# Moving loads to ScalarE's queue and stores to SyncE's in a planned attention-and-mixer kernel, with later assumed transposes, a third output buffer and no TensorE turning

## The chip, the cores and the metric

One core of one Trainium2 chip runs the whole program. The metric is device time in microseconds of one execution, inputs and outputs in HBM. The medians are of several executions. All executions here carry the state "fast" (one core, no other core to disturb it); the kernel before nevertheless spreads over 17 us, and that spread turns out to be part of the story.

Names used: PE is TensorE (PEld its weight loads), DVE is VectorE, ACT is ScalarE, POOL is GpSimd, SP is SyncE.

## The reference

Eight batches of a gated attention without softmax, followed by a mixer:

```python
# batch 8, S = 3136, D = 256, d_qk = 64, rank 32, hidden 1024
scores = z @ z.T / S                       # symmetric, per batch
x      = u * (maximum(scores, 0)**2 @ v)
h      = (x.T @ U @ V).T                   # low-rank mixing over the sequence
uu     = x + h
out    = uu + maximum(uu @ w_ch1, 0) @ w_ch2
```

The scores are symmetric, so a 128x128 block computed for (row, column) serves (column, row) once it is transposed. Most blocks are transposed by DMA, on SP.

## The kernel before

The program is planned in Python before it is built. Every piece of work is a task with engines, an assumed duration and an assumed latency. A small simulation of the engines picks at each moment which task each engine takes, and the resulting order is emitted. The engines run it in order and wait on semaphores. So a changed assumption costs nothing by itself: it changes the order of the same work.

```python
LQ = "SP"; SQ = "POOL"            # queues of loads and stores
TURNED = tuple(range(8,16))       # batch 0: block rows that TensorE transposes
Z_AT1 = 2; V_AT1 = 5              # column of batch 0 after which z, v of batch 1 are fetched
AT24_0 = 6                        # place of the tail column in batch 0
L_PE, L_EW, L_TR, L_DMA = 0.36, 0.08, 1.3, 2.2   # assumed latencies; L_TR: DMA transpose
LTR0 = 1.0                        # more of it in batch 0
...
x = add(f"tr{b}.{c}.{t0}", {"SP": t_tr(nt)}, ..., pipe=TB * nt,
        lat=L_TR + (LTR0 if b == 0 and c >= 8 else 0.0))     # transpose by DMA
...
add(f"st{b}.{k}.{h}", {SQ: 0.6 if SQ == "POOL" else 0.45} if b < NB - 1 else {"SP": 0.5}, ...)
...
def gate_v(self, t, v):           # POOL: one element, holds back the three cast loads of v (batch 0)
    i = self.nc.gpsimd.tensor_copy(out=w[:1, NT // 2, :1], in_=w[:1, 2 * GATE_V, :1])
```

Half of batch 0's v is loaded by three POOL DMAs that cast to bf16 on the way; both kernels do so. `gate_v` waits until the first v piece is cast, so that these loads don't compete with the first z and v.

## Time and profile before

| | before |
|---|---|
| median of the first three runs | 1040.89 us (1038.57 to 1045.36) |
| profiled execution | 1035.29 us, span 1033.5 us |
| TensorE busy, idle | 1011.2 us, 22.3 us |
| idle TensorE in the first 75 us | 8.8 us |
| DVE, ACT, POOL busy | 590.8, 498.9, 73.0 us |

The busy share of TensorE counts a matmul from its start to its modelled end, so it includes filling and draining. "Granted clock" is the share of TensorE's full clock that the chip let it run at. The page says where TensorE is idle, and the table of stretches says when. Those lines are in the prediction below.

### The profile page before, as it was taken

Reading aid. Unit: us, or ns where it says so; the run is one execution under the profiler, and the core shown is the slowest. Engines: PE = TensorE matmul, PEld = TensorE weight load, DVE = VectorE, ACT = ScalarE, POOL = GpSimd, SP = SyncE. Lnnn points to the kernel's source line nnn. Section 1 sums busy time; section 2 is a strip of 40 time slices with the busy share of each in tenths; the row PEclk is TensorE's granted clock in tenths of the full one; section 3 lists DMA queues with packets and bytes.
Section 4 is the critical chain, followed back from the end, with each engine's and each line's share of the span. In section 5 each row is a group of like instructions: output and inputs, shape, how many; then the busy total and the mean of one; then the engine's idle time right before and its main releaser. Section 6 shows DMA issues by size and latency. Waiting matters only on the chain.

```text
span 1033.5 us, 22358 instructions
## 1 busy us (share of the span) xinstructions
PE 1011.2 (98%) x9164; PEld 749.7 (73%) x9243; DVE 590.8 (57%) x1054; ACT 498.9 (48%) x614; POOL 73.0 (7%) x137
## 2 busy tenths in 40 slices
PE   8899999999999999999999999999999999999998
PEld 5578777777777777777677777677767777678765
DVE  8796754457645646465564656565654565443352
ACT  7664554544454445453463445544454453552343
POOL 1060000000000000001000000000000000000000
PEclk9899999999999999999999999999999999999999
DMA  9989998889888888897897979889898789663152
GB/s 214 182 218 212 153 197 199 188 176 171 178 202 177 181 152 188 189 202 153 158 194 179 199 170 179 165 206 199 145 181 200 185 167 180 130 129 89 39 123 83
DMA packets 408103, 176.41 MB, mean 171 GB/s; under 512 B 369824, under 2 KB 373216, under 8 KB 408000
## 3 DMA queue, kind: packets, MB, share of 16 engines
q1 hardware_dynamic: 400112, 151.32, 73.3%
q0 software_dynamic: 7600, 23.27, 6.9%
q8 instruction: 72, 1.18, 0.5%
q10 hardware_dynamic: 288, 0.39, 0.1%
q14 instruction: 31, 0.25, 0.1%
HBM read 60.70 MB, written 25.69 MB: 84 GB/s over the span
## 4 chain that ended last, share of the span: by engine, by line
PE 92%; DMA 4%; DVE 2%; issue 1%; ACT 1%; SPq 0%; POOL 0%; DVEq 0%; POOLq 0%; ACTq 0%
PE acc L1124 47%; PE acc L1268 16%; PE pair L1242 15%; PE pair L1087 7%; PE acc L1134 2%; DMA uT<-ubf 1%; DMA q<-q 1%; PE acc L1139 1%; PE pair L1204 1%; DVE q L1108 1%; PE acc L1166 1%; PE acc L1261 1%; DMA us<-in_u_dram 0%; DVE q L1215 0%; DMA stg<-in_moe_U_dram 0%
## 5 line engine op out<-in xcount | busy, mean ns | idle before, releaser
L1124 PE MATMUL acc<-v,q 128*128 128x256 bf16 x4632 | 569.2, 273 | 5.0 <-DMA q<-TJ 1.8
L1124 PEld LDWEIGHTS <-q 128*128 128x128 bf16 x4632 | 441.8, 98 | 121.2 <-issue 41.7
L1102 ACT ACTIVATE q<-pair 128x1024 bf16<-128x1024 f32 (+7 forms) x268 | 217.8, 863 | 183.4 <-PE pair L1087 180.4
L1253 ACT ACTIVATE r<-pair 128x1024 bf16<-128x1024 f32 (+1 forms) x191 | 187.4, 1009 | 193.1 <-PE pair L1242 184.4
L1108 DVE TENSOR_TENSOR q<-q 128x1024 bf16<-128x1024 bf16 (+7 forms) x392 | 211.6, 579 | 10.1 <-ACT q L1102 8.3
L1268 PE MATMUL acc<-w2b,r 128*128 128x256 bf16 x1536 | 181.6, 273 | 0.6 <-DVE xc L1157 0.6
L1157 DVE TENSOR_TENSOR xc<-acc,us 128x256 bf16<-128x256 f32 x192 | 80.9, 422 | 171.3 <-PE acc L1134 83.9
L1242 PE MATMUL pair<-uT,w1b 128*128 128x512 bf16 (+1 forms) x711 | 165.8, 350 | 5.9 <-DMA uT<-ubf 2.1
L1268 PEld LDWEIGHTS <-r 128*128 128x128 bf16 x1536 | 148.7, 98 | 26.9 <-issue 6.9
L1104 DVE TENSOR_SCALAR q<-pair 128x768 bf16<-128x768 f32 (+6 forms) x124 | 119.4, 968 | 79.5 <-PE pair L1087 72.6
L1242 PEld LDWEIGHTS <-w1b 128*128 128x128 bf16 x896 | 78.9, 98 | 70.2 <-issue 6.8
L917 POOL DMA_DIRECT2D out_dram<-ob x98 | 53.4, 545 | 860.1 <-DVE ob L1280 776.8
L1087 PE MATMUL pair<-zT 64*128 64x384 bf16 (+4 forms) x952 | 99.7, 313 | 0.9 <-DVE q L1104 0.4
L1280 DVE TENSOR_TENSOR ob<-acc,u 128x512 f32<-128x512 f32 (+1 forms) x91 | 60.0, 659 | 62.2 <-PE acc L1268 61.9
L1215 DVE TENSOR_TENSOR u<-pair,xc 128x1024 f32<-128x1024 f32 x42 | 50.8, 1219 | 11.9 <-PE pair L1204 11.9
L1087 PEld LDWEIGHTS <-zT 64*128 64x128 bf16 x952 | 35.3, 95 | 30.5 <-issue 20.8
L943 ACT CAST ubf<-u 128x1024 bf16<-128x1024 f32 x25 | 26.2, 1046 | 49.6 <-DVE u L1215 38.1
L947 DVE CAST v<-stg 128x512 bf16<-128x512 f32 (+1 forms) x58 | 24.2, 418 | 41.5 <-DMA stg<-in_v_dram 41.5
L943 ACT CAST v<-stg 128x512 bf16<-128x512 f32 (+1 forms) x40 | 24.2, 605 | 33.5 <-DMA stg<-in_v_dram 33.0
L1134 PE MATMUL acc<-v,q 64*128 64x256 bf16 (+1 forms) x168 | 26.9, 277 | 0.0
L1242 PE MATMUL pair<-q,w1b 128*128 128x512 bf16 (+1 forms) x106 | 22.0, 351 | 1.6 <-DVE q L1215 1.0
L973 ACT ACTIVATE zbf<-stg 128x512 bf16<-128x512 f32 (+1 forms) x26 | 15.3, 613 | 11.6 <-DMA stg<-in_z_dram 11.6
(78 smaller groups left out, 242.8 us busy)
## 6 DMA issues: line engine op xcount, KB each, us to landing
us<-in_u_dram SPq DMA_DIRECT2D x96, 256.0 KB, 3.4
stg<-in_v_dram SPq DMA_DIRECT2D x90, 256.0 KB, 3.6
out_dram<-ob POOLq DMA_DIRECT2D x84, 256.0 KB, 3.4
q<-q SPq DMA_TRANSPOSE x356, 3.3
stg<-in_z_dram SPq DMA_DIRECT2D x22, 256.0 KB, 3.3
out_dram<-ob SPq DMA_DIRECT2D x12, 256.0 KB, 2.0
stg<-in_moe_w_ch_dram SPq DMA_DIRECT2D x8, 256.0 KB, 4.1
v<-in_v_dram POOLq DMA_DIRECT2D x3, 256.0 KB, 8.6
```

Source lines behind the costliest of these rows:

```text
L917: i = self.q_of(t).dma_start(out=out, in_=in_)
L1087: self.nc.tensor.matmul(out=ps[:, h, pc : pc + w], lhsT=z[a, r * P : (r + 1) * P], rhs=z[a, c0 : c0 + w], start=True, stop=True,)
L1102: self.nc.scalar.activation(out=o, in_=i, func=AF.Relu)
L1104: self.nc.vector.tensor_single_scalar(out=o, in_=i, scalar=0.0, op=ALU.max)
L1108: self.nc.vector.tensor_tensor(out=o, in0=o, in1=o, op=ALU.mult)
L1124: self.nc.tensor.matmul(out=self.acc[acc.i][:, d0 : d0 + D], lhsT=self.q[:, ref.i, :], rhs=self.v[v.i][:, j, :], start=first and n == 0, s ...
L1157: self.nc.vector.tensor_tensor(out=o, in0=i0, in1=i1, op=ALU.mult)
L1215: self.nc.vector.tensor_tensor(out=o, in0=i, in1=x, op=ALU.add)
L1242: self.nc.tensor.matmul(out=o, lhsT=self.w1b[:, e, ht * P : (ht + 1) * P], rhs=r, start=e == 0, stop=e == ND - 1)
L1253: self.nc.scalar.activation(out=o, in_=i, func=AF.Relu)
L1268: self.nc.tensor.matmul(out=self.acc[acc.i][:, w * D : (w + 1) * D], lhsT=self.r1[r1s[ht // 2].i][:, ht % 2, (2 * h + w) * P : (2 * h + w ...
L1280: self.nc.vector.tensor_tensor(out=o, in0=i, in1=x, op=ALU.add)
```

## The change

The intent: take load issues off SP, where transposes are issued, put stores there instead of on POOL, and let the plan expect transposes later. Several settings were retuned with it.

```diff
-LQ = "SP"
-SQ = "POOL"
-DIRECT = (0, 20, 16, 20)
+LQ = "ACT"
+SQ = "SP"
+DIRECT = (0,20,16,20,22)
-TURNED = tuple(range(8,16))
-W_AT = 6
+W_AT = 5
-Z_AT1 = 2
-V_AT1 = 5
+Z_AT1 = 7
+V_AT1 = 7
-AT24_0 = 6
+AT24_0 = 4
-LTR0 = 1.0
-LOOK = 8
+LTR0 = 2.0
+L_TR = 2.5
+LOOK = 10
-NEAR = 1
+NEAR = 3
-HOLD = 0.06
+HOLD = 0.03
 ... (Z_AT 5 to 4, TOKS 5 to 6; buffers: "ob" 2 to 3, score blocks 296 to 288; one small memset doubled)
-                    f"zt{b}.{p}", {"PE": 0.06 * nb}, ...
+                    f"zt{b}.{p}", {"PE": (0.056 if b else 0.107) * nb}, ...
 ... (the branch for TURNED, turn_quad and copy_quad are removed)
```

More of the change, by code (lines that the diff above doesn't have):

```diff
@@ L21 @@
 ZSCALE = 1.0 / math.sqrt(float(S))
-NBLK = 296
 NXC = 7
+NUS = 3
+NSTG = 6
+NUT = 2
+NR1 = 7
+NOB = 3
+NBLK = 296 - 8 * (NXC + NUS + NSTG + NUT + NR1 + NOB - 27)
 NPAIR, NACC = 3, 2
-LQ = "SP"
-SQ = "POOL"
-DIRECT = (0, 20, 16, 20)
+LQ = "ACT"
+SQ = "SP"
+DIRECT = (0,20,16,20,22)
 FLIP = 16
+ZB = 1
 WARM = 22
-TURNED = tuple(range(8,16))
-W_AT = 6
+W_AT = 5
 W_ST = 1.5
-Z_AT1 = 2
-V_AT1 = 5
+Z_AT1 = 7
+V_AT1 = 7
 V_ST1 = 1.0
-Z_AT = 5
+Z_AT = 4
 GATE_V = 0
-TOKS = 5
-AT24_0 = 6
+TOKS = 6
+AT24_0 = 4
 AT24 = 4
@@ L50 @@
 TR = 0.3
-LTR0 = 1.0
-LOOK = 8
+LTR0 = 2.0
+L_TR = 2.5
+L_EW = 0.08
+L_DMA = 2.2
+LOOK = 10
 SOFT = 5
-NEAR = 1
+NEAR = 3
 ACCS = 3
-HOLD = 0.06
+HOLD = 0.03
 HOLD_LAST = 0.14
@@ L114, in t_tr @@
     return 1.25 + 0.03 * nb
-L_PE, L_EW, L_TR, L_DMA = 0.36, 0.08, 1.3, 2.2
+L_PE = 0.36
 class Plan:
@@ L331, in make_plan @@
     for name, n in (
-        ("xc", NXC), ("pair", NPAIR), ("acc", NACC), ("stg", 6), ("us", 3),
-        ("zbf", 2), ("zT", 2), ("v", 2), ("TJ", 1), ("o24", 1), ("u24", 1), ("x24", 2), ("u32", 3), ("ubf", 1), ("uT", 2),
-        ("r1", 7), ("r24", 1), ("ob", 2), ("t1", 2), ("t1f", 1), ("tok", TOKS),
+        ("xc", NXC), ("pair", NPAIR), ("acc", NACC), ("stg", NSTG), ("us", NUS),
+        ("zbf", 2), ("zT", 2), ("v", 2), ("TJ", 1), ("o24", 1), ("u24", 1), ("x24", 2), ("u32", 3), ("ubf", 1), ("uT", NUT),
+        ("r1", NR1), ("r24", 1), ("ob", NOB), ("t1", 2), ("t1f", 1), ("tok", TOKS),
     ):
@@ L376, in make_plan @@
             ), 0.1)
-            if b:
+            if b >= ZB:
                 ztr.append(add(
@@ L387, in make_plan @@
                 m = add(
-                    f"zt{b}.{p}", {"PE": 0.06 * nb}, lambda K, t, z0=z0, nb=nb, zbf=zbf, pr=pr: K.mm_z(t, z0, nb, zbf, pr),
+                    f"zt{b}.{p}", {"PE": (0.056 if b else 0.107) * nb}, lambda K, t, z0=z0, nb=nb, zbf=zbf, pr=pr: K.mm_z(t, z0, nb, zbf, pr),
                     deps=[c0, c1], kind="z", alloc=[pr], use=[zbf],
@@ L530, in make_plan @@
                 src = [TJ] if parts is None else refs if flip else [refs[r0 - t0 + i] for i in range(nt)]
-                if b == 0 and parts is not None and (-1 if flip else c) in TURNED:
-                    pr = Ref("pair")
-                    m = add(
-                        f"pt{b}.{c}.{t0}", {"PE": 0.107 * nt + 0.02},
-                        lambda K, t, src=src, nt=nt, pr=pr: K.turn_quad(t, src[0], nt, pr),
-                        deps=[s], kind="z", alloc=[pr], use=src,
-                    )
-                    x = flex(add(
-                        f"pc{b}.{c}.{t0}", {"DVE": t_dve(nt * P), "ACT": t_act(nt * P)},
-                        lambda K, t, tb=tb, nt=nt, pr=pr: K.copy_quad(t, tb, nt, pr),
-                        deps=[m], prio=0.95, use=[pr] + tb.refs,
-                    ), 0.6)
-                else:
-                    x = add(
-                        f"tr{b}.{c}.{t0}", {"SP": t_tr(nt)},
-                        lambda K, t, src=src, tb=tb, nt=nt, o=t0 * 64: K.tr_quad(t, src[0], o, tb, nt),
-                        deps=[s], prio=0.5, pipe=TB * nt, use=src + tb.refs, lat=L_TR + (LTR0 if b == 0 and c >= 8 else 0.0),
-                    )
+                x = add(
+                    f"tr{b}.{c}.{t0}", {"SP": t_tr(nt)},
+                    lambda K, t, src=src, tb=tb, nt=nt, o=t0 * 64: K.tr_quad(t, src[0], o, tb, nt),
+                    deps=[s], prio=0.5, pipe=TB * nt, use=src + tb.refs, lat=L_TR + (LTR0 if b == 0 and c >= 8 else 0.0),
+                )
             for n, (r, i) in enumerate(tiles):
@@ L866, in __init__ @@
         self.x24 = many("x24_", 2, [P, P], BF16)
-        self.stg = many("stg", 6, [P, 512], FP32)
-        self.us = many("us", 3, [P, 2, D], FP32)
+        self.stg = many("stg", NSTG, [P, 512], FP32)
+        self.us = many("us", NUS, [P, 2, D], FP32)
         self.zbf = many("zbf", 2, [P, 8, P], BF16)
@@ L877, in __init__ @@
         self.ubf = many("ubf", 1, [P, ND * 4 * P], BF16)
-        self.uT = many("uT", 2, [P, ND * 4 * P], BF16)
+        self.uT = many("uT", NUT, [P, ND * 4 * P], BF16)
         self.ubt = sb.tile([P, P], BF16, name="ubt")
-        self.r1 = many("r1_", 7, [P, 2, 512], BF16)
+        self.r1 = many("r1_", NR1, [P, 2, 512], BF16)
         self.r24 = many("r24_", 1, [P, NH, 192], BF16)
-        self.ob = many("ob", 2, [P, 2, D], FP32)
+        self.ob = many("ob", NOB, [P, 2, D], FP32)
         self.t1sb = many("t1_", 2, [P, D], BF16)
@@ L896, in __init__ @@
         nc.vector.tensor_copy(out=self.identf, in_=self.ident)
+        nc.vector.memset(self.zbt[64:], 0.0)
         nc.vector.memset(self.zbt[64:], 0.0)
@@ L1111, in tr_quad @@
         self.chain(self.nc.sync.dma_start_transpose(out=self.q[:, tb.i : tb.i + nt, :], in_=self.cols(src, off, nt * P)))
-    def turn_quad(self, t, src, nt, pr):
-        ps = self.pair[pr.i].rearrange("p a b -> p (a b)").bitcast(BF16)
-        for n in range(nt):
-            self.nc.tensor.transpose(out=ps[:, n * P : (n + 1) * P], in_=self.q[:, src.i + n, :], identity=self.ident)
-    def copy_quad(self, t, tb, nt, pr):
-        ps = self.pair[pr.i].rearrange("p a b -> p (a b)").bitcast(BF16)
-        self.copy(t, self.q[:, tb.i : tb.i + nt, :].rearrange("p t r -> p (t r)"), ps[:, : nt * P])
     def av(self, t, seg, acc, v, d0, first, last):
```

## The prediction

> **What bounds the kernel now.** I read the busy shares on the page first, then the chain that ended last, then the page's slices, and last the waits of single engines and short stretches of the trace.
>
> ```profile
> PE 1011.2 (98%) x9164; PEld 749.7 (73%) x9243; DVE 590.8 (57%) x1054; ACT 498.9 (48%) x614; POOL 73.0 (7%) x137
> ...
> PEclk9899999999999999999999999999999999999999
> DMA  9989998889888888897897979889898789663152
> ...
> PE 92%; DMA 4%; DVE 2%; issue 1%; ACT 1%; SPq 0%; POOL 0%; DVEq 0%; POOLq 0%; ACTq 0%
> ```
>
> TensorE (PE) has work in flight for 98% of 1033.5 us, and 92% of the chain is its matmuls. It is idle for 22.3 us in all. Where, the table of stretches tells (us, then busy time of PE, PEld, DVE, ACT and POOL, granted clock, DMA share, GB/s):
>
> ```profile
> 0.00:25.00 25.00, 21.96 (x201) 14.41 (x202) 20.09 (x42) 19.88 (x27) 2.88 (x10) 1.00 0.93 215
> 25.00:50.00 25.00, 20.41 (x199) 12.96 (x197) 18.59 (x34) 15.78 (x24) 0.00 (x0) 0.86 0.98 173
> 50.00:75.00 25.00, 23.82 (x217) 17.78 (x216) 23.28 (x42) 16.18 (x22) 16.80 (x29) 1.00 0.93 232
> ...
> 225.00:250.00 25.00, 25.00 (x305) 20.04 (x304) 17.39 (x31) 10.11 (x14) 2.17 (x4) 1.00 0.88 167
> ```
>
> The first 75 us hold 3.0 + 4.6 + 1.2 = 8.8 us of the idle time, with a clock of 0.86 in the second row. The end (last matmul, one addition, one store) holds about 4, and the last batch about 3 more. From 100 to 850 us TensorE idles about 4 us in 750. So nearly all that can be won lies in the first batch.
>
> A 98% busy TensorE is not at its peak: in the middle of the run 24 matmuls of 256 columns take 2.62 us in the chain (109 ns each), yet the group of 4632 takes 569.2 us, 123 ns each. The difference is filling and draining the pipeline when the work switches between attention, scores and the mixer. The change keeps the kinds of work and so, I assume, most of these switches.
>
> **What the Trainium skill says.**
> 1. "Perfetto Trace Analysis", Identifying the Most-Contended Engine: matmul busy share is no measure of nearness to the roof; the weight-load share is better. Here that is 73%, which agrees with the 109 against 123 ns: some room is left inside the 98%, but only for a change of matmul order.
> 2. "DMA: Bandwidth & Descriptors", Issuing engines are not separate DMA queues: SP, ACT and POOL feed the same 16 DMA engines, and spreading saves only issue time. The trace before has a DMA share of 0.83 to 0.98 nearly throughout, so I expect no bandwidth from a second queue, only issue time.
> 3. "TensorE: Matmul & The Clock Gate", Part 1: the array's clock falls when it idles and comes back after sustained work. The trace agrees: at 30 to 35 us TensorE is busy 2.71 of 5 us and the granted clock is 0.52; at 35 to 40 us it is busy all the time at 0.80. That costs 5 x 0.48 + 5 x 0.20 = 3.4 us at most beside the idle time.
> 4. "Perfetto Trace Analysis", DMA Instruction - HWDGE: the sequencer holds the descriptor generator exclusively while it makes descriptors. If SP and ACT share one, a load on ACT waits behind a transpose on SP. The trace before cannot tell: ACT issues only two loads, of 0.41 and 0.45 us, at a time without transposes.
>
> **Part by part.**
>
> *Loads to ACT, stores to SP.* Durations of issues from the view of the one helper line:
>
> ```profile
> L917 SPq DMA_DIRECT2D stg<-in_v_dram x98: 327/571/1604, 2.3 to 840.8; - x98
> L917 POOL DMA_DIRECT2D out_dram<-ob x98: 538/542/577, 133.3 to 986.3; - x98
> L917 SPq DMA_DIRECT2D us<-in_u_dram x96: 323/430/1576, 8.6 to 945.2; - x96
> ...
> L1111 SPq DMA_TRANSPOSE q<-q x350: 1125/1240/4557, 11.3 to 935.3; - x175
> ```
>
> SP carries 259 loads; by the diff some 15 of batch 0 stay (7 of v, 3 of z, 5 of u). To ACT go about 91 of v at 0.57, 93 of u at 0.43, 28 of z at 0.57, 14 small ones at 0.55 and 18 weight loads at 0.4: 52 + 40 + 16 + 8 + 7 = 123 us. ACT goes from 499 us (48%) to about 622 us (60%) of occupied time. SP loses those 123 us and takes 98 stores at about 0.35 to 0.57 (34 to 55 us), so it is relieved by some 70 to 90 us; its 366 transposes at 1.24 us (454 us) stay. POOL loses 53 us, which cost nothing. ACT now idles about 180 us for scores and 184 us for the mixer, and TensorE almost never waits for ACT (about 1 us in all). A load of 0.5 us ahead of an eviction delays it, but the order of instructions is planned with 0.45 us for a load, and three PSUM pairs stand between. I put +2 us on it.
>
> *Transposes assumed to land later (2.5 us for 1.3).* Measured is 3.3 us from issue to landing. What TensorE and its weight loads wait for transposes is small:
>
> ```profile
> PEld L1124 <- DMA q<-TJ: 2.1, 1, 2.1
> PE pair L1242 <- DMA uT<-ubf: 2.1, 2, 1.4
> ...
> PE acc L1124 <- DMA q<-TJ: 1.8, 1, 1.8
> ```
>
> The truer latency puts other matmuls first. The uT waits are worth 2.1 us; I take -1.5. In batch 0 the tail column also moves from place 6 to 4: its 50 small matmuls (two pieces of 0.89 us) need no transpose and can fill the 1.8 us wait for q<-TJ at 28.8 us. If so, part of the clock dip goes as well. Of 4.3 us idle at 25 to 35 us and 3.4 us of clock I take -4.
>
> *No blocks turned by TensorE.* Gone are 44 matmuls of 128 columns, 8 PSUM copies and the waits in front:
>
> ```profile
> L1116 PE MATMUL pair<-ident,q 128*128 128x128 bf16 x44 | 3.6, 220 | 1.4 <-DVE q L1108 1.0 <-ACT q L943 0.4
> ...
> L947 DVE COPY q<-pair 128x768 bf16<-128x768 bf16 (+3 forms) x7 | 3.1, 502 | 0.0
> ```
>
> At half the 109 ns of a 256-column matmul that is 2.4 us of TensorE and 1.4 us of waits, hence -3.8. In their place come 8 more DMA transposes, 10 us on SP at 1.24 us, between about 38 and 58 us, where the DMA share is already about 1. The z and v loads of the next batch, which stand there now, move back by five and two columns and make room. In the short views the zT<-zbf transposes at 43.7 us took 4.1 us, so rows 8 to 15 may land 4 to 6 us after issue; the plan allows 2.5 + 2.0. Some of it will be missed: +3.
>
> *One more direct step for columns 16 to 19.* Two score matmul pairs of 512 columns: +0.5 us. The third output buffer: in steady state the additions wait for TensorE (61.9 us of 62.2), not for a store, so 0. It costs eight blocks of 296, again taken as 0.
>
> Sum: +2 - 1.5 - 4 - 3.8 + 3 + 0.5 = -3.8 us. Free changes of matmul order (a deeper look-ahead, another hold) are worth some us either way and I cannot sign them. From 1040.9 that gives 1037; I lean 2 us lower for the tuning that visibly went with it: 1035.
>
> **The rivals.**
> (a) *ACT becomes the hidden bound.* An in-order ACT waits at a load for its buffer or for the descriptor generator and evictions come late. If each of 244 loads took 1.0 us instead of 0.5, ACT would rise to about 740 us (72%), and TensorE would stall at score bursts; 0.1 us per load gives +24 us and a time near 1060. For: transposes fill SP for over 45% of the time, and loads on SP took up to 1.6 us. Against: ACT has 360 us of slack and the two ACT issues seen were short.
> (b) *The start turns DMA-bound.* The eight transposes come late, columns 9 to 15 wait, and the clock falls again: two more dips like the one at 30 us, +8 to +12 us, a time near 1048. For: DMA share 0.93 to 0.98 in the first 75 us. Against: the prefetch is moved out of the way.
> (c) *Transfers are hidden anyway.* Everything outside batch 0 is bound by TensorE at 24.9 of 25 us; only the 3.8 us of the turning go: 1037, "the same".
> (d) *The bubbles shrink.* A better matmul order reclaims 2 us per batch of switching: 1020.
>
> **Range and chances.** (c) and my sum agree within a few us and get most weight; (d) sets the low end, (a) and (b) the high end. Three runs before spread over 7 us, which belongs in the range too: 1020 to 1053. Faster by over 2% means below 1020.1, which needs nearly all 22 us of idle time or (d): 0.11. Slower by over 2% means above 1061.7, which needs (a) in full: 0.08. Within 2%: 0.81.
>
> **What would show it.** Right: TensorE busy 97 to 99%, about 9120 matmuls, no L1116 group; first 75 us with 5 to 8 us idle and a clock above 0.9 at 25 to 50 us; ACT issues near 0.5 us; stretches from 225 to 850 us still 24.8 of 25. Wrong: waits of TensorE for ACT over 10 us or ACT issues over 0.8 us (a); new waits of L1124 for q<-q before 80 us (b); the same busy share but a span below 1020 with the group of 4632 well under 569 us (d).

## The result and the profile after

The changed kernel takes **1032.51 us** (median of 6, 1031.40 to 1035.34). The kernel before, run beside it, has 1044.57 us (median of 6, 1038.57 to 1046.13). The ratio is 0.990, 95% interval 0.987 to 0.993: "the same" at the 2% mark, but clearly 1% faster. Ratios are computed as the mean time of one kernel's fast runs over that of the other's of the same rounds, so they are not quite the ratio of the medians.

The page of the changed kernel, the line of busy shares:

```profile
PE 1013.0 (98%) x9205; PEld 747.1 (72%) x9205; DVE 601.6 (58%) x1075; ACT 481.6 (47%) x592; POOL 19.5 (2%) x39
```

TensorE has as much work in flight as before. The 9205 records are those of the weight loads before (9243), less the 44 turning matmuls, plus 6 for scores. (I had started from 9164 matmul records, some of which are missing.) The page's busy time of ACT, which leaves out DMA issues, did not grow: 481.6 us for 498.9. ACT's 246 issues take another 93.5 us, so that it is occupied for about 575 us where the prediction had 622. The first stretches (columns as in the prediction's table):

```profile
0.00:25.00 25.00, 21.52 (x192) 14.23 (x193) 18.71 (x42) 18.50 (x24) 3.65 (x10) 0.93 0.90 210
25.00:50.00 25.00, 22.61 (x218) 14.92 (x217) 21.48 (x37) 17.43 (x23) 1.89 (x4) 0.93 1.14 193
50.00:75.00 25.00, 24.28 (x216) 18.23 (x214) 21.15 (x38) 12.02 (x18) 13.97 (x26) 1.00 1.16 218
```

Idle here: 3.5 + 2.4 + 0.7 = 6.6 us, for 8.8 before. The waits of TensorE over the whole run:

```profile
PE pair L1232 <- DMA uT<-ubf: 3.2, 3, 1.2
...
PE pair L1086 <- ACT q L1101: 1.1, 2, 0.5
```

The issues on ACT (nanoseconds, minimum/median/maximum, then first and last start):

```profile
L916 ACTq DMA_DIRECT2D us<-in_u_dram x93: 329/335/726, 32.2 to 942.6; - x93
L916 ACTq DMA_DIRECT2D stg<-in_v_dram x91: 329/335/636, 70.0 to 831.7; - x91
```

The chain that ended last is of no use here: for this run it breaks off after 4% of the span.

**Where the time went.** The batch's first low-rank matmul needs all columns of its batch, so its start marks a batch's end. The table gives the start of the first of them (batch 0) and of the last batch's last one, and the count of attention matmuls in the first 100 us (one stretch, restricted to that line). All numbers are of the profiled execution.

| run | time of that execution, us | end of batch 0 | end of batch 7 | between | attention matmuls by 100 us |
|---|---|---|---|---|---|
| before | 1035.3 | 109.4 | 974.7 | 865.3 | 540 |
| before_again | 1046.9 | 116.5 | 986.3 | 869.8 | 485 |
| changed | 1033.0 | 104.8 | 972.1 | 867.3 | 580 |
| after_again | 1032.1 | 103.5 | 971.2 | 867.7 | 585 |

The seven batches in between take the same time within 4.5 us. What remains after them is 58.8 us before and 59.1 us after. The lead is made in the first batch: about 5 us against a quick execution of the kernel before (of which 2 are lost again in between), 12 us against a slow one. Of the quick 4.7 us, 3.0 are less work of TensorE before the end of batch 0 (97.6 us busy for 100.6; the turning took 3.6) and 1.7 less idle time (7.1 us for 8.8).

### The profile page after: what moved, and what is told of

Read it like the earlier page. It is cut to its first block, busy times and chain, and to the rows that moved or that the text cites. A ratio compares the mean times of both kernels' runs of the same rounds, so it can differ in the third digit from the quotient of the medians.

```text
span 1031.2 us, 22253 instructions
## 1 busy us (share of the span) xinstructions
PE 1013.0 (98%) x9205; PEld 747.1 (72%) x9205; DVE 601.6 (58%) x1075; ACT 481.6 (47%) x592; POOL 19.5 (2%) x39
## 5 line engine op out<-in xcount | busy, mean ns | idle before, releaser
L1101 ACT ACTIVATE q<-pair 128x1024 bf16<-128x1024 f32 (+7 forms) x276 | 220.4, 846 | 257.7 <-PE pair L1086 240.5
L1107 DVE TENSOR_TENSOR q<-q 128x1024 bf16<-128x1024 bf16 (+7 forms) x395 | 214.4, 579 | 13.1 <-ACT q L1101 11.5
L1232 PE MATMUL pair<-uT,w1b 128*128 128x512 bf16 (+1 forms) x784 | 168.2, 353 | 3.2 <-DMA uT<-ubf 3.2
L1103 DVE TENSOR_SCALAR q<-pair 128x768 bf16<-128x768 f32 (+7 forms) x119 | 119.4, 1004 | 55.6 <-PE pair L1086 45.5
L942 ACT CAST ubf<-u 128x1024 bf16<-128x1024 f32 x23 | 24.0, 1045 | 43.1 <-DVE u L1205 39.9
L946 DVE CAST v<-stg 128x512 bf16<-128x512 f32 (+1 forms) x71 | 28.8, 408 | 20.5 <-DMA stg<-in_v_dram 20.3
L942 ACT CAST v<-stg 128x512 bf16<-128x512 f32 (+1 forms) x27 | 16.4, 613 | 12.1 <-DMA stg<-in_v_dram 12.0
L1124 PEld LDWEIGHTS <-q 64*128 64x128 bf16 (+1 forms) x168 | 11.4, 95 | 12.2 <-issue 10.5
L1245 DVE TENSOR_SCALAR r<-pair 128x1024 bf16<-128x1024 f32 (+1 forms) x9 | 10.0, 1106 | 15.2 <-PE pair L1232 13.0
```

The lines of the kernel that those rows point to most:

```text
L942: self.nc.scalar.copy(out=out, in_=in_)
L1101: self.nc.scalar.activation(out=o, in_=i, func=AF.Relu)
L1103: self.nc.vector.tensor_single_scalar(out=o, in_=i, scalar=0.0, op=ALU.max)
L1107: self.nc.vector.tensor_tensor(out=o, in0=o, in1=o, op=ALU.mult)
L1232: self.nc.tensor.matmul(out=o, lhsT=self.w1b[:, e, ht * P : (ht + 1) * P], rhs=r, start=e == 0, stop=e == ND - 1)
```

## The experiments

Twelve runs were made, two of them of the unchanged kernels. Names beginning with b_ start from the kernel before, those with a_ from the changed one.

### before_again and after_again: the two kernels unchanged

> The kernel before, unchanged, to get the span and the granted clock of each execution: its profiled run took 1035.3 us although the median of six runs was 1044.6, while the changed kernel's profile and median agree (1033.0 and 1032.5). Theory A (the difference is made by the first batch and its clock dips): executions that take 1044 us show a mean granted clock lower than the 0.997 of the profiled one, by up to 0.01. Theory B (the difference is made by the route of the stores or loads, so by transfers): the clock is 0.996 to 0.998 in all executions whatever they take. Ratio to the kernel before 1.000 within 0.003 under both.

> The changed kernel, unchanged, as the base of the other runs of this call. Expected 1031 to 1036 us in every execution (it had 1031.4 to 1035.3), where the kernel before has two groups, near 1035 and near 1045. Ratio to the kernel before 0.988 to 0.995, depending on how many executions of before fall into its late group.

Measured: before_again 1039.22 us (1035.55 to 1046.89, ratio 0.999), after_again 1031.88 us (1031.19 to 1032.17, ratio 0.992, interval 0.989 to 0.995). I have 42 executions of the kernel before with their clocks: 15 under 1039 us (mean granted clock 0.997), 11 from 1039 to 1042 (0.996), 16 above 1042 (0.994), with a mean of 1041.1. Ten of the changed kernel lie between 1031.2 and 1035.3, mean 1032.4. So theory A's sign is there: slow executions have a lower clock. The 15 quick executions average 1036.7. By this cut, about half of the mean lead of 8.7 us is the absence of slow executions (1041.1 to 1036.7), the rest a better course of the others (1036.7 to 1032.4). The 42 times have no clear gap, and another cut gives another share.

The slow start, stretches of before_again:

```profile
0.00:25.00 25.00, 16.37 (x147) 10.79 (x148) 18.04 (x38) 15.98 (x22) 4.74 (x10) 0.96 0.99 178
25.00:50.00 25.00, 21.42 (x172) 12.89 (x172) 16.99 (x30) 15.71 (x20) 0.00 (x0) 0.83 0.97 168
```

TensorE is idle 8.6 us in the first stretch where the quick execution had 3.0. It waits for v:

```profile
PE acc L1124 <- DMA v<-in_v_dram: 6.0, 2, 4.7
```

The three cast loads landed 13.8 us after issue at the median, 8.6 us in the quick execution. Why they were issued late is in the timelines of POOL and DVE (start, duration). The quick execution's copy first, then the slow one:

```profile
8.49 0.39 POOL L1014 COPY v<-v 1x1 bf16<-1x1 bf16 x1 [7.18 <-ACT v L943]
...
8.52 2.26 POOL L1014 COPY v<-v 1x1 bf16<-1x1 bf16 x1 [7.21 <-ACT v L943]
11.10 1.78 POOL L917 DMA_DIRECT2D v<-in_v_dram  x3 [0.31 <-POOL v L1014]
```

```profile
8.19 1.28 DVE L1108 TENSOR_TENSOR q<-q 128x1024 bf16<-128x1024 bf16 x2
9.39 0.41 DVE L947 CAST v<-stg 128x512 bf16<-128x512 f32 x1
9.73 0.68 DVE L1108 TENSOR_TENSOR q<-q 128x1024 bf16<-128x1024 bf16 x1
10.33 0.41 DVE L947 CAST v<-stg 128x512 bf16<-128x512 f32 x1
10.66 1.21 DVE L947 CAST zT<-pair 128x1024 bf16<-128x1024 f32 x1
```

The one-element copy took 2.26 us. It ended at 10.78 us, 0.12 us after DVE went from an unbroken row of SBUF-to-SBUF work to a cast out of PSUM. The page "SBUF — State Buffer" of the Trainium skill, A bandwidth-pool intuition that's wrong, states for a POOL DMA beside a DVE copy that it is "blocked until DVE-end + ~115 ns", because DVE holds their shared port. For this copy the trace agrees in kind: its wait ends with DVE's row. It does not test the 115 ns, since the last SBUF operation ended at 10.74 us by the trace (10.33 + 0.41), only 0.04 us before the copy did. In b_stores_sp and b_lat_new too the copy took 2.15 and 2.33 us and ended 0.12 to 0.13 us after that PSUM cast began. In before and b_loads_act it slipped in within 0.39 and 0.36 us, in b_both_queues within 0.71, although DVE's row was the same. When it is late, the loads go out at 11.1 us instead of 9.2, 0.2 us before SP begins its transposes at 11.3. They go out 1.9 us later and land 7.1 us later. That the transposes delay them is argued from the times: in the three traces with 0.2 us between the two the loads took 12.6 to 14.3 us, in the other ten that have the gate, with 1.5 us or more between them, 7.4 to 10.2.

The changed kernel's plan has DVE's PSUM cast ahead of the v casts. This is after_again:

```profile
8.88 1.21 DVE L946 CAST zT<-pair 128x1024 bf16<-128x1024 f32 x1
```

```profile
8.83 0.18 POOL L1013 COPY v<-v 1x1 bf16<-1x1 bf16 x1 [7.52 <-ACT v L942]
```

The row is shorter: the PSUM cast follows at once on two TENSOR_TENSOR, so POOL cannot wait for long. In the other trace of the changed kernel its copy began beside these two, took 0.45 us and again ended 0.13 us after the cast began. In all seven traces of the changed kernel and its variants the copy took at most 0.45 us, and the loads landed within 9.1 us at the median. So the times coincide in all thirteen traces that have the gate. That DVE's order decides it is argued from this and not shown: no run changed that order alone. Nor does the late copy make the whole of a slow execution: before_again is 11.6 us longer than before, of which 7.0 us arise in the first batch and 4.5 us later.

### b_stores_sp, b_loads_act, b_both_queues: only the queues

```diff
 def dma(self, t, out, in_):
-    i = self.q_of(t).dma_start(out=out, in_=in_)
+    q = <sync for stores> / <scalar for the moved loads> / self.q_of(t)
+    i = q.dma_start(out=out, in_=in_)
```

> The kernel before with only the stores issued from SP instead of POOL, at the same places of the planned order; every other engine keeps its instructions and their order. Theory A (order of the matmuls and first batch make the 1%): nothing or slightly slower, ratio 0.998 to 1.004, because a store now stands in SP's line in front of transposes. Theory B (stores through POOL slow something that the profiled run did not show): ratio 0.990 to 0.994, the whole gain.

> The kernel before with only the loads of the changed set issued from ACT instead of SP, at the same places of the planned order. Theory A: ratio 0.999 to 1.004; ACT's issues 0.4 to 0.6 us each, TensorE's waits for ACT up by 1 to 3 us, its waits for transposes down by 1 to 2 us. Rival of the prediction (ACT becomes the hidden bound): ratio 1.01 or more and issues of 0.8 us or more. Theory B': loads and transposes in two rings let transposes land sooner, ratio 0.993 to 0.997.

> The kernel before with both moves of queues and its own order of everything. Theory A: ratio 0.998 to 1.005, so the queues alone give nothing and the gain of 1% needs the new plan. Theory B: ratio 0.988 to 0.993, the gain comes from the queues alone.

| run | median, us | ratio | 95% interval |
|---|---|---|---|
| b_stores_sp | 1051.76 | 1.0103 | 1.0052 to 1.0153 |
| b_loads_act | 1040.91 | 0.9997 | 0.9950 to 1.0045 |
| b_both_queues | 1046.34 | 1.0059 | 1.0008 to 1.0110 |

Theory B falls: the queues alone win nothing. Loads on ACT cost nothing that this resolves (half a per cent, 5 us). Their issues took 0.335 us (median) for both u and v. Stores on SP cost 1% in the old order, more than theory A allowed. The waits of TensorE in b_stores_sp:

```profile
PE pair L1244 <- DMA uT<-ubf: 8.0, 7, 2.5
...
PE acc L1270 <- DVE xc L1159: 4.9, 5, 1.6
```

and the waits of SP's queue in the same run:

```profile
SPq L1113 <- DVE q L1110: 106.9, 71, 7.1
SPq L919 <- DVE ob L1282: 67.3, 30, 9.2
```

In the kernel before, where only the last batch's 14 stores are on SP, the second wait is already there, at half the size:

```profile
SPq L917 <- DVE ob L1280: 32.6, 16, 4.9
```

This is the likely mechanism: SP stands at a store until DVE's addition is done, 67 us in 30 waits for 33 us in 16. The transposes behind it, the mixer's uT among them, go out late: TensorE waits 8.0 us for uT, 2.1 and 3.5 in the two traces of the kernel before. The plan of this run believed the stores to be on POOL, so nothing in its order allowed for that. The place fits: from the end of batch 0 to the end of batch 7, where the stores are, this execution took 878.6 us, and the kernel before 865.3 and 869.8. Its late v at the start, with TensorE waiting 6.7 us, is not the stores' doing.

### a_stores_pool: the changed kernel's stores back on POOL

```diff
+        st = t.name[:2] == "st" and t.name[2] != str(NB - 1)
+        q = self.nc.gpsimd if st else self.q_of(t)
```

> The changed kernel with its stores of batches 0 to 6 issued from POOL again, at the same places of the order. Theory D (stores among the transposes cost time on SP in any plan; the new plan only hides most of it): 2 to 6 us faster than the changed kernel, TensorE's wait for uT down from 3.2 us to about 1. Rival (the longer assumed latency hides the stores entirely): within 1.5 us of the changed kernel.

Measured: 1032.32 us (1028.22 to 1034.45), ratio 0.992 as after_again. The rival holds: in the new order the stores on SP cost nothing measurable (the interval is 0.988 to 0.996), although in the changed kernel SP waits 71.3 us for the additions, and here 34.6. A plan that puts stores into SP's own line and expects transposes later hides them.

### b_no_gate: without POOL's one-element copy

```diff
     def gate_v(self, t, v):
+        return
```

> The kernel before without the one-element copy on POOL that holds back its three cast loads of v; the loads then go out after the identity is made, near 1.5 us, and everything else keeps its order. Theory C (the two groups of executions come from a race at the start: when POOL's copy takes 2.3 us instead of 0.4 the v loads go out behind the first transposes, land 14 instead of 9 us later and the clock falls): no execution over 1040 us, median 1034 to 1038, ratio 0.992 to 0.997, v loads land before the first transpose is issued at 11 us. Rival (the late group comes from elsewhere): still two groups, ratio 0.998 to 1.002. The early loads may delay the first z and v by 1 us.

Measured: 1042.28 us (1039.74 to 1045.47), ratio 1.002. Theory C as I put it fails: the v loads went out at 1.45 us and landed 7.2 us later, but the spread stayed. The stretches of 5 us show what replaced it: TensorE was busy 1.48 of 5 us from 5 to 10 us and its clock was 0.50 in the next 5. The early loads took DMA from the first z and v, which is what the gate is for. So the late gate goes with a slow start in three traces, and taking the gate away gives a start that is slow in another way. The four executions still fall into two pairs (1039.7 and 1039.8, 1044.7 and 1045.5): that the spread of the kernel before comes from the gate is not shown.

### a_lat_old and b_lat_new: the assumed latency alone

```diff
 # a_lat_old                 # b_lat_new
-L_TR = 2.5                  -L_TR 1.3
+L_TR = 1.3                  +L_TR 2.5
-LTR0 = 2.0                  -LTR0 = 1.0
+LTR0 = 1.0                  +LTR0 = 2.0
```

> The changed kernel planned with the old assumption on transposes (1.3 us, and 1.0 more in the first batch). Theory D: the longer assumption is what pays for the stores on SP, so this is 6 to 12 us slower than the changed kernel, near 1042, with TensorE's waits for uT at 6 us or more. My prediction on record: 1.5 us slower. A new plan moves everything a little, so 2 us either way are no sign.

> The kernel before with only the assumption on transposes changed (2.5 us for 1.3, and 2.0 for 1.0 more in the first batch): loads stay on SP, stores on POOL, two output buffers, eight rows turned by TensorE, all other settings old. Theory E (the assumed latency is the change that counts, whatever the queues): 1028 to 1035 us, ratio 0.987 to 0.995, TensorE's waits for uT near 1 us. Rival F (the old plan with loads and stores out of the way of SP had no need of it, and the latency only pays in the new one): 1037 to 1043 us, ratio 0.997 to 1.003.

a_lat_old: 1047.29 us (1038.98 to 1049.54), ratio 1.0045 where after_again has 0.992. Its waits of TensorE:

```profile
PE pair L1232 <- DMA uT<-ubf: 6.9, 6, 2.1
PE pair L1086 <- DMA zT<-zbt: 5.4, 1, 5.4
```

The first is theory D's. The second is new: at the change from batch 0 to batch 1 TensorE waits for the last piece of z, which all a_ kernels fetch late (`Z_AT1 = 7`), this one latest. Its transpose is issued at 87.7 us, at 79.5 and 82.2 in the two traces of the changed kernel, and at 54.5 before. The stretch there, with the clock falling after the gap:

```profile
75.00:100.00 25.00, 19.65 (x178) 15.33 (x177) 13.62 (x33) 7.15 (x13) 0.00 (x0) 0.86 0.90 211
```

That is 5.4 us idle and at most 3.5 us of clock (25 x 0.14). Batch 0 ends at 116.2 us.

b_lat_new: 1050.34 us, ratio 1.007 (1.001 to 1.013). Theory E falls, and so does rival F's "no effect": the longer assumption alone does not help the old settings. TensorE's uT waits do fall, to 0.9 us, but its profiled execution had the late v at the start (12.6 us to landing), and a wait of 5.8 us for DVE later.

### a_turned: rows 8 to 15 turned by TensorE again

```diff
+TURNED = tuple(range(8,16))
+                if b == 0 and parts is not None and (-1 if flip else c) in TURNED:
+                    m = add(f"pt{b}.{c}.{t0}", {"PE": 0.107 * nt + 0.02}, ... K.turn_quad ...)
+                    x = flex(add(f"pc{b}.{c}.{t0}", {"DVE": ..., "ACT": ...}, ... K.copy_quad ...), 0.6)
```

> The changed kernel with rows 8 to 15 of the first batch turned by TensorE again (44 matmuls, 8 copies, 8 DMA transposes fewer). The prediction on record put removing them at -3.8 us of TensorE and waits and +3 us of late transposes, so this should be 0 to 2 us slower than the changed kernel's 1031.9: 1032 to 1034. Rival (the turning had been useful where DMA is full): 2 to 4 us faster, 1028 to 1030. A new plan moves things by some us by itself.

Measured: 1042.06 us (1040.09 to 1043.99), ratio 0.999. That is 10 us slower than after_again, not 0 to 2. It was run at another time. Against the kernel before the difference is 0.7%, or 7 to 8 us. All four executions lie above all ten of the changed kernel. Batch 0 ends at 112.2 us, 7 to 9 us later. The turning itself:

```profile
L1129 PE MATMUL pair<-ident,q 128*128 128x128 bf16 x44 | 3.5, 219 | 0.1
L960 DVE COPY q<-pair 128x896 bf16<-128x896 bf16 (+3 forms) x7 | 3.4, 518 | 0.3 <-PE pair L1129 0.3
```

The matmuls run at 0.056 us (7 in 0.39 us), 2.4 us in all, and nothing waits long. The copies fall where DVE is full:

```profile
50.00:75.00 25.00, 24.87 (x227) 18.76 (x226) 24.49 (x42) 14.21 (x23) 11.48 (x23) 1.00 0.89 201
```

DVE is busy 24.5 of 25 us here, for 21.2 in the changed kernel and 22.6 in after_again. But TensorE is busy for 24.87 us of the same stretch, and up to the end of batch 0 it is idle for 6.8 us, no more than in the changed kernel's traces (7.1 and 6.2). So a full DVE does not hold TensorE up here. Batch 0 ends later because more work stands before its end: 988 weight loads for 906. Of these 82, 44 turn blocks, and the others are nearly all attention and score matmuls of batch 1. TensorE idles more only afterwards: 11.4 us between the two ends, for 4.1 and 7.6, with waits of 2.7 us for uT and 2.6 us for an output buffer among them. Why the plan with turning comes to these is open.

### a_at24_6: the tail column back at place 6

```diff
-AT24_0 = 4
+AT24_0 = 6
```

> The changed kernel with the tail column of the first batch back at place 6 instead of 4. The prediction on record put most of the gain at 25 to 35 us on this move (-4 us with the clock). If right: 1034 to 1037 us, TensorE waits for q<-TJ again at about 28 us. If the move was without effect, as the first 50 us of the changed kernel with its dip of the clock at 25 to 35 us suggest: 1031 to 1033.

Measured: 1041.06 us (1034.97 to 1043.13), ratio 0.996 (0.989 to 1.004). Its median is some 9 us above after_again's, but hardly for my reason. It was run at another time. By the ratios the difference is 0.4%, or 4 to 5 us, within overlapping intervals, and one of the four executions is as fast as the changed kernel. The wait for q<-TJ is 0.8 us. The larger one is again the last z of batch 1:

```profile
PE pair L1086 <- DMA zT<-zbt: 3.9, 1, 3.9
```

In this run its transpose was issued at 86.1 us; TensorE's clock was 0.50 from 95 to 100 us.

### a_replan: the same settings, another order

```diff
-    return 0.18 + n * 0.000834
+    return 0.185 + n * 0.000834
```

> The changed kernel planned anew with one constant moved that the change does not touch: the planned fixed time of an ACT instruction, 0.185 for 0.180 us. All settings of the change stay; only the order that the plan gives to the same work differs, from early in the first batch on. Three single undoings of the changed kernel each took 1041 to 1047 us, undoing parts of opposite kind. Theory G (the changed kernel is one favourable order among many, and planning anew loses most of its lead whatever is altered): 1038 to 1046 us, new waits of TensorE of 3 us or more somewhere. Theory H (each undone part was really worth 9 to 15 us): 1030 to 1034 us, as the changed kernel. In between, 1034 to 1038, a part of the losses of the three runs is the new order and a part is what was undone.

Measured: 1031.98 us (1029.18 to 1037.41), ratio 0.9915 (0.987 to 0.996). Theory G falls: an order that differs from early in batch 0 on keeps the whole lead. So making the plan anew does not by itself lose the lead. That the undoings above lost theirs only by what was undone is likely but not shown: the largest wait of a_at24_6, for the last z, is a matter of order. The waits that G expected did come, 4.1 us for uT at 124.5 us, without costing the lead. One control does not measure the spread of such orders, and this one's executions spread twice as wide as the changed kernel's; differences of 2 us between re-planned kernels I do not read.

No run beat the changed kernel clearly. The lowest single time, 1028.22 us, is of a_stores_pool, whose ratio is the same.

## Why the prediction was right or wrong

The number and the class held: 1032.5 us lies in 1020 to 1053, within 2%. By its own steps:

- **TensorE is the bound, and what can be won lies in the first batch.** Right. From the end of batch 0 to the end of batch 7 both kernels need 865 to 870 us, and TensorE is busy 24.8 to 24.9 of 25 us from 225 to 850 us.
- **Loads to ACT, +2 us.** The issue time was oversized. The step took durations measured on SP (0.57 and 0.43 us); on ACT both took 0.335 at the median, so the 123 us of issue became about 93. The effect was 0 within half a per cent (b_loads_act, 0.9997), which leaves the +2 us themselves unresolved. Rival (a) is out: 24 us would have shown.
- **Stores to SP, no cost counted, SP "relieved".** Wrong as a term of its own. It counted SP's issue time and not its standing at a store: in the old order +1.0%. In the new order it is 0.
- **Later transposes, -1.5 us from the uT waits.** The failed size. Those waits did not shrink (2.1 and 3.5 us in the two traces before, 3.2 and 3.0 after), but without the assumption the changed kernel is 15 us slower at the median. The step read the assumption as a saving over the old waits; by a_lat_old it is what makes the other parts affordable.
- **Turning removed, -3.8 +3.** TensorE's share was sized right (2.4 us), and up to the end of batch 0 the kernel has 4.7 us less of work and idle time. But putting the turning back into the new plan costs 7 to 10 us where the step's sum said 0.8, and the idle time comes after batch 0, which the step did not look at. The +3 was not paid: the q<-q transposes issued from 30 to 60 us did land late, 4.2 and 5.4 us after issue at the median of the two traces (3.3 before; the step had 4 to 6), but TensorE waited for none of them. Rival (b) is out.
- **Tail column, -4 us at 25 to 35 us.** The wait for q<-TJ did vanish and the first 75 us idle 6.6 us, within my 5 to 8. The clock dip stayed: 0.93 in one profile but 0.86 in the other. Undoing the move cost 4 to 9 us, mostly elsewhere.
- **Three output buffers, 0.** Not tested.
- **The sum.** The terms cannot be added at all. Undoing three parts singly costs 9, 10 and 15 us by the medians (5, 8 and 13 by the ratios), in sum well over the total lead of 9. The prediction's range survived because the bound held every sum near the same time. That its centre, 1035, came within 3 us is luck: terms were missed in both directions.
- **What it did not see.** The kernel before has slow executions. The profiled one was among the quickest, so its 8.8 us of idle at the start understated what was to be won: a slow one is idle for 8.6 us in the first 25 us alone. By the cut at 1039 us, about half of the mean lead is the absence of slow executions.

## What to carry to other kernels

When the profiled execution is faster than the median, profile again before trusting its list of waits; the start of a kernel may have two courses. In a statically planned kernel the assumed latencies belong to the queue assignment: here SP stood at stores until additions were done, and the transfers behind them came late unless the plan knew. Effects of settings tuned together should be tested by undoing one at a time beside a re-planned control, and not be added up.

## What the Trainium skill lacked or had wrong

- "Perfetto Trace Analysis", DMA Instruction — HWDGE, says the descriptor generator is shared by two sequencers and locked while it is used. In the changed kernel SP issues 364 q<-q transposes (1.24 us each at the median). The 36 loads of v on ACT that overlapped the issue of a transpose on SP took 0.336 us at the median, the other 55 took 0.334; for the loads of u (tile `us`) it is 0.335 (68) and 0.334 (25). No load of the two kinds took more than 0.73 us, and on SP, before, those of v took 0.571 at the median. No wait of one for the other shows.
- "SBUF — State Buffer", A bandwidth-pool intuition that's wrong, tells of one DVE operation. Here a row of DVE operations followed each other so closely that a one-element POOL copy waited through several of them, 2.15 to 2.33 us for 0.18 to 0.71, in some executions and not in others. The page does not say that the outcome can change from run to run of the same order.
- "DMA: Bandwidth & Descriptors", Issuing engines are not separate DMA queues, says that another issuer only saves issue time. That section leaves out that an issuer also carries its waits to what stands behind: with the stores on SP its waiting for additions went from 33 to 67 us, and the kernel took 1% longer.
